# A linear-attention, Mish and greedy-mixture kernel: the token assignment moved off GpSimd, the first expert's weights converted in small pieces, and the front end's order adjusted

## The chip, the cores and the metric

The kernel runs on one core of a Trainium2 chip. The core has a matrix engine (TensorE, PE in the profile; PEld is its weight load), a vector engine (VectorE, DVE), a scalar engine (ScalarE, ACT), GpSimd (POOL) and a queue engine that issues transfers (SyncE, SP). Each engine works through its own instructions strictly in program order, and waits on semaphores for the others. The metric is the device time of one execution in microseconds (us). Before the change it is 855.05 us, the median of three runs (854.58 to 855.65).

## The reference

Three stages follow each other. All data are float32.

```python
# 1. linear attention: batch 4, 8 heads, 768 steps, head size 48
for t in range(S):
    cur = einsum('bhd,bhe->bhde', u * kt, vt)
    y[:, :, t] = einsum('bhd,bhde->bhe', rt, state + cur)
    state = wt[..., None] * state + einsum('bhd,bhe->bhde', kt, vt)
x = y as (3072 tokens, 384)
# 2. h = x @ w_in (384 x 2048);  g = h * tanh(softplus(h));  x = g @ w_out (2048 x 384)
# 3. greedy mixture: 8 experts of 384 x 1024 and 1024 x 384, room for 384 tokens each
order = argsort(-(x @ w_gate).flatten())
for idx in order:                      # the largest logit first
    tok, e = idx // 8, idx % 8
    if assigned[tok] >= 0 or counts[e] >= 384: continue
    assigned[tok] = e; counts[e] += 1
out[assigned == e] = relu(x[...] @ w1[e]) @ w2[e]
```

Every matrix product with float32 accuracy is made of three float16 products: each factor is split into a high and a low half (hi, lo), and hi·hi, hi·lo and lo·hi are summed.

## The kernel before, in words

**Stages 1 and 2 as one list of events.** The attention is cut into 24 units of 128 steps (4 sequences, 6 chunks each). A unit has the steps att0 (running product of the decays), inv, r1, k1, bon1 and bon2 (the u term), K and S (state), A1 (scores) and y. The Mish layer works on 12 groups of 256 tokens; a group has eight slots, each a first product (mm1: 18 matmuls into a tile Hp), followed by the activation steps aln, tanh and g. Its second product (mm2) is a stream of 384 portions of three matmuls into a tile X; `more(n)` emits the next n portions, wherever it is called. The weights of the Mish layer arrive as raw words and are converted (`conv`, on the vector engine) and split into halves (`split`, on ACT and the vector engine), and w_out's blocks are transposed and multiplied by the gate weights (ogT, ogM), which gives the logits as eight further columns of the second product. Each step is an event with a due time from the table `CFG`; the events are sorted by due time (units are 4 slots apart: `at(4 * n - 13 + o, ...)`), and called in that order, so the table alone decides the order on every engine. `warm` events are matmuls without use, `need` only checks at build time that a step comes after those it rests on. The tile Y of the attention has two buffers, which bon1, bon2, K, S and y take in turn.

**The gate.** When the event list is done, 128 or a few fewer portions of the second product are left, and `gate()` works out which token goes to which expert. It takes seven phases. A phase finds the threshold at which the next expert is full, by a search with 32 candidates at a time: four iterations (`count`) in phase 0, three in each of the other six, 22 in all. In an iteration the vector engine compares 3072 keys with 32 candidates in two halves (L854), TensorE counts by 24 small matmuls (`tally`, L859), the vector engine compares the counts with the room left (ge, L871), TensorE spreads the result (bc, L874), and the vector engine reduces it (L875) and forms the next keys (L921). Wherever such a step hands over to another engine the generator yields, and the main loop calls `more(CFG["amount"][kind])`: nine matmuls behind the first half of the compare, three behind the tally, nine between phases ('c'), twelve at each of the steps 't' of the set-up and of `make_idx`. At the end of a phase, `assign` multiplies the one-hot rows by the selection and adds them to Acc, on GpSimd (L902, L904).

**The first expert's weights** are fetched before the gate (`load_w(0)`, two transfers of 1.5 MB into tiles stg, two buffers each used once per expert) and converted during it: at every fourth yield, `conv_w(..., pool=True)` has ACT write the high half (L1105) and GpSimd scale the weights and write the low half (L1107, L1108), a third of a matrix at a time. Behind the gate `load_w(1)` fetches the second expert into the same buffers.

**make_idx** turns the assignment into a list of tokens per expert: one-hot rows OH (24 instructions, L1074), and a table Q times the token numbers tid (on GpSimd, L1069), multiplied on TensorE (L1079). The rest of the stream is spread over its four yields 'o'. **The experts:** GpSimd gathers the tokens' rows (L1115), a register is loaded and tested (L1199 to 1203; the branch to an exact gate is not taken here), and for each expert the rows are transposed (`xpose`, L1127), multiplied (L1148, L1165) and scattered.

Of the kernel before, what the change touches and what calls it, by code (L numbers as in the profile page):

```python
# [9 lines left out]
F32 = mybir.dt.float32  # L10
# [3 lines left out]
ALU = mybir.AluOpType  # L14
# [4 lines left out]
P = 128  # L19
# [4 lines left out]
CFG = {'conv': [-27.9, -26.2, -0.2, 0.8, 1.8, 2.8, 3.7, 5.3, 5.9, 6.6, 7.3, 8.0, 8.7, 10.4, 10.6, 11.3],  # L24
 'split': [-27.3, -25.6, 0.9, 1.9, 2.9, 3.8, 4.7, 5.7, 6.7, 7.4, 8.1, 8.8, 9.0, 11.2, 11.4, 12.1],
 'ogT': [7.5, 8.45, 9.9, 10.25, 10.95, 11.85, 12.55, 13.25],
 'ogM': [8.15, 9.35, 10.2, 10.9, 11.35, 12.05, 12.75, 14.45],
 'u': {'att0': -0.5,
       'bon1': 2.27,
       'bon2': 3.25,  # L30
       'r1': 2.7,
       'k1': 3.175,
       'K': 4.91,
       'A1': 5.52,
       'S': 5.93,
       'y': 6.8,
# [16 lines left out]
            'K': -17.4,  # L53
            'A1': -18.5,
            'bon2': -18.5,
# [13 lines left out]
            'inv': -22.8,  # L69
            'r1': -17.5,  # L70
            'bon1': 2.3,
            'k1': -17,
            'bon2': 3.05,
            'K': 3.85,
            'A1': 3.7,
            'S': 4.05,
            'y': 5.5},
        4: {'K': 4.96,
            'A1': 5.82,
            'S': 5.98,  # L80
            'y': 7.0,
# [26 lines left out]
        7: {'bon1': 1.37,  # L108
            'att0': -0.4,
            'bon2': 4.35,  # L110
# [10 lines left out]
        23: {'K': 3.81, 'A1': 6.27, 'y': 6.65}},  # L121
 'rate': [(9, 0), (81, 200), (82, 202), (85, 216), (86, 220), (93, 234), (99, 256)],
 'close_cv': 15.0,
 'close_att': 86.65,
 'mm1': 0.7,
 'mm2': 1.4,
 'aln': -0.1,
 'tanh': (1.6, 1.66),
 'g': (3.0, 3.01),
# [7 lines left out]
           ('ld', 9): -23.6,  # L137
           ('warm', 1): -26.45,
           ('warm', 2): -24.4,
# [3 lines left out]
           ('warm', 6): 9.9},  # L143
 'warm': [36, 0, 12, 0, 0, 0, 0],
 'amount': {'I0': 3, 'I1': 0, 'g': 1, 't': 4, 'c': 3, 'o': 11},
 'cwn': 4,
 'dve': {'glo': {0,
# [59 lines left out]
 'alone': {9},  # L207
 'lg': 4.01}


@with_exitstack
def tile_rwkv_mish_greedy_moe(
# [12 lines left out]
    nc = tc.nc  # L225
# [4 lines left out]
    NCH = SEQ // C  # L230
# [51 lines left out]
    def part(n, i):  # L282
        if i == 0:
            return TB[n % 3][:, 0:WC].rearrange("p (a c) -> p a c", a=NP)
        return TB[n % 3][:, WC + (i - 1) * RC:WC + i * RC].rearrange("p (a c) -> p a c", a=NP)
# [70 lines left out]
    def need(*keys):  # L356
        assert made.issuperset(keys), keys
# [491 lines left out]
    NH = 2  # L849
# [11 lines left out]
    def count(x, E_, gr, mid=None, late=None):  # L861
        cn = pgs.tile([J, NE], F32, name="cn")
        for h in range(NH):
            compare(x, gr, h)
            if h == 0 and mid is not None:
                mid()
            yield f"I{h}"
            tally(cn, E_, h)
        if late is not None:
            late()  # L870
        nc.vector.tensor_tensor(ge, cn, remS[0:J, :], op=ALU.is_ge)  # L871
        yield "g"
        bc = pgs.tile([P, NE], F32, name="tp", bufs=1)
        nc.tensor.matmul(bc, ones[0:J, :], ge, start=True, stop=True)  # L874
        nc.vector.tensor_reduce(nn_, bc, op=ALU.max, axis=AX.X)  # L875
        cnt_out[:] = [cn, bc]

    cnt_out = [None, None]

    def setup_range():  # L880
# [19 lines left out]
    def assign(ph, E_, s_):  # L900
        dst = Acc if ph == 0 else Ap
        nc.gpsimd.tensor_tensor(dst, E_, s_[:, :, None].to_broadcast([P, NTT, NE]), op=ALU.mult)  # L902
        if ph > 0:
            nc.gpsimd.tensor_tensor(Acc, Acc, Ap, op=ALU.add)  # L904

    def gate():
# [6 lines left out]
        for ph in range(NE - 1):  # L913
# [25 lines left out]
            nc.vector.tensor_tensor(cur, best, tk, op=ALU.add)  # L939
            assign(ph, E_, s_)  # L940
            yield "c"
# [111 lines left out]
    def make_idx(middle=None):  # L1053
# [8 lines left out]
        with nc.allow_low_precision(reason="slots are integers below 2^24"):  # L1062
# [5 lines left out]
                                slf[:, 0, :, None].to_broadcast([P, NTT, NTT]), op=ALU.is_equal)  # L1068
        nc.gpsimd.tensor_tensor(Q, Q, tid[:, :, None].to_broadcast([P, NTT, NTT]), op=ALU.mult)  # L1069
        ix = pgs.tile([P, NTT], F32, name="cn")  # L1070
        NQ = 4
        for q in range(NQ):
            for i in range(q * NTT // NQ, (q + 1) * NTT // NQ):
                nc.vector.tensor_scalar(OH[:, i], col, slf[:, 1, i:i + 1], None, op0=ALU.is_equal)  # L1074
            if q == 0 and middle is not None:
                middle()
            yield "o"
            for i in range(q * NTT // NQ, (q + 1) * NTT // NQ):
                nc.tensor.matmul(ix, OH[:, i, :], Q[:, i], start=(i == 0), stop=(i == NTT - 1))  # L1079
# [13 lines left out]

    def conv_w(e, step, pool=False):
        s1, s2 = wts[e]
        if step == 0:
            wf[e] = tuple(p2b[e % 2].tile(sh, F16, name=nm, bufs=1)
                          for sh, nm in (([P, 2, KD, F2], "a1"), ([P, 2, NF2, DM], "a2")))
        a1, a2 = wf[e]
        if step < KD:  # L1100
            src, dst, sc_ = s1[:, step], a1[:, :, step], SW1
        else:
            h = slice(3 * (step - KD), min(3 * (step - KD) + 3, NF2))
            src, dst, sc_ = s2[:, h], a2[:, :, h], SW2
        nc.scalar.activation(dst[:, 0], src, AF.Copy, scale=sc_)  # L1105
        if pool:
            nc.gpsimd.tensor_scalar(src, src, sc_, 1.0, op0=ALU.mult, op1=ALU.mult)  # L1107
            nc.gpsimd.tensor_tensor(dst[:, 1], src, dst[:, 0], op=ALU.subtract)  # L1108
        else:
            nc.vector.scalar_tensor_tensor(dst[:, 1], src, sc_, dst[:, 0], op0=ALU.mult, op1=ALU.subtract)  # L1110

# [67 lines left out]
    load_w(0)  # L1179
    cw = [(0, i) for i in range(NCV)]  # L1180
    amount = CFG["amount"]
    n = 0
    for kind in gate():
        more(amount[kind])
        n += 1
        if n % CFG["cwn"] == 0 and cw:
            conv_w(*cw.pop(0), pool=True)
    for x in cw:
        conv_w(*x, pool=True)
    load_w(1)  # L1190
    for kind in make_idx(check):
# [8 lines left out]
    with tc.If(redo > 0):  # L1200
        exact_gate()
        run_through(make_idx())
        gather(0)
    for e in range(NE):
        nx = e + 1 < NE
# [83 lines left out]
```

## Time and profile before

| what | value |
| --- | --- |
| time, median of 3 runs | 855.05 us |
| the profiled execution's own time | 854.59 us |
| its span | 852.8 us |
| busy PE / DVE / ACT / POOL | 778.8 / 536.1 / 518.5 / 88.9 us |
| mean granted TensorE clock | 0.961 |

The profile shows one execution. The span goes from the first instruction to the last; 1.8 us of the execution's time lie outside it. A busy time is the sum of the instructions of an engine; PE is busy for 91% of the span, but that is a mean over stages with different limits. The granted clock is 1 at TensorE's higher level (2.4 GHz) and 0.5 at its lower (1.2 GHz); a mean between them says how a stretch was divided. Times in the rows below are counted from the start of the span; a row of a timeline holds the start, the length, engine, line, operation and tiles, and in brackets the idle time of that engine before it and what ended it.

### The profile page before, as it was taken

The page shows a single profiled execution, that of the slowest core. Times are in us where ns is not written, and L with a number is a line of the kernel's source. Part 1 is how long each engine was busy: PE and PEld are TensorE (multiplying, and loading weights), DVE is VectorE, ACT ScalarE, POOL GpSimd, SP SyncE. Part 2 cuts the span into 40 slices and gives each one's busy share as a digit, 9 for nine tenths or more (in the row PEclk, how much of TensorE's full clock was granted, in tenths as well). Part 3 has the DMA queues.
Part 4 walks back from the last instruction along what each step waited for, and adds up shares of the span by engine and source line. Part 5 has one row for each costly group of instructions (what it writes and reads, how often), then busy time and mean ns, then how long its engine had stood idle before and what let it go on. Part 6 is the DMA issues. An engine that isn't in the chain of part 4 may idle for free.

```text
span 852.8 us, 16533 instructions
## 1 busy us (share of the span) xinstructions
PE 778.8 (91%) x7047; PEld 538.0 (63%) x7047; DVE 536.1 (63%) x861; ACT 518.5 (61%) x731; POOL 88.9 (10%) x123
## 2 busy tenths in 40 slices
PE   7683879999999999999999999799959999999996
PEld 3562656777777777767776775455536556555564
DVE  6999875767677767676765345766655543455520
ACT  2558879898988888888977794110005543355521
POOL 0000000000000000000000002531130232122311
PEclk9796999999999999999999999899979999999999
DMA  7870412222322223322200004000144444555100
GB/s 281 211 234 11 149 38 53 38 52 65 71 41 50 52 48 68 69 44 49 50 25 11 15 1 168 10 20 20 46 179 158 147 136 163 185 194 185 65 29 28
DMA packets 21822, 73.79 MB, mean 87 GB/s; under 512 B 4112, under 2 KB 12688, under 8 KB 19696
## 3 DMA queue, kind: packets, MB, share of 16 engines
q1 hardware_dynamic: 18672, 63.24, 25.1%
q0 software_dynamic: 3072, 9.44, 3.5%
q8 instruction: 57, 0.93, 0.5%
q14 instruction: 21, 0.17, 0.1%
HBM read 62.05 MB, written 9.44 MB: 84 GB/s over the span
## 4 chain that ended last, share of the span: by engine, by line
PE 50%; issue 18%; DVE 13%; ACT 12%; POOL 5%; DMA 0%; POOLq 0%; ACTq 0%; DVEq 0%
PE X L639 18%; PE Hp L587 15%; POOL xr L1115 3%; POOL out_dram L1170 2%; PE A L439 2%; PE Y L491 2%; PE Y L495 2%; ACT es L607 2%; PE cn L859 2%; ACT L590 1%; PE A L375 1%; ACT L606 1%; PE Hp L1148 1%; ACT es L590 1%; DVE cv L516 1%
## 5 line engine op out<-in xcount | busy, mean ns | idle before, releaser
L639 PE MATMUL X<-wo,g 128*128 128x392 f16 (+1 forms) x1152 | 223.4, 337 | 1.7 <-DVE V L681 0.9
L587 PE MATMUL Hp<-xg,wi 128*128 128x256 f16 x1728 | 209.4, 276 | 3.0 <-DVE wi L527 2.0
L587 PEld LDWEIGHTS <-wi 128*128 128x128 f16 x1728 | 168.8, 99 | 35.5 <-issue 3.1
L639 PEld LDWEIGHTS <-g 128*128 128x128 f16 x1152 | 108.4, 100 | 68.9 <-issue 12.1
L1148 PE MATMUL Hp<-xe,a 128*128 128x384 f16 (+1 forms) x612 | 102.6, 322 | 6.3 <-DVE hT L1153 5.2
L1165 PE MATMUL X<-a,hT 128*128 128x384 f16 x576 | 97.2, 326 | 0.0
L590 ACT ACTIVATE es<-Hp 128x512 f32<-128x512 f32 x96 | 57.9, 603 | 56.7 <-PE Hp L587 56.2
L1148 PEld LDWEIGHTS <-a 128*128 128x128 f16 x612 | 59.5, 100 | 48.2 <-issue 14.2
L608 DVE TENSOR_TENSOR hs<-hs,es 128x1024 f32<-128x1024 f32 x48 | 56.8, 1220 | 41.2 <-ACT es L607 41.2
L1165 PEld LDWEIGHTS <-hT 128*128 128x128 f16 x576 | 56.4, 98 | 34.8
L1153 DVE SCALAR_TENSOR_TENSOR hT<-Hp,hT 128x384 f16<-128x384 f32 x64 | 35.3, 552 | 47.6 <-ACT hT L1152 47.6
L366 ACT ACTIVATE x1o<-X 128x384 f32<-128x384 f32 x21 | 10.4, 497 | 89.4 <-PE X L639 61.9
L621 DVE TENSOR_TENSOR g<-hs,g 128x1024 f16<-128x1024 f32 x48 | 56.6, 1220 | 12.4 <-ACT g L366 12.2
L1168 ACT ACTIVATE or<-X 128x384 f32<-128x384 f32 x24 | 11.8, 490 | 81.0 <-issue 60.7
L366 ACT ACTIVATE hs<-Hp 128x512 f32<-128x512 f32 x92 | 55.4, 602 | 0.0
L1105 ACT ACTIVATE a<-stg 128x1024 f16<-128x1024 f32 (+2 forms) x48 | 49.9, 1048 | 7.3 <-DMA stg<-in_w_dram 7.3
L802 POOL IOTA jk<- 128x32 f32 x5 | 0.6, 154 | 509.3 <-PE Hp L587 509.3
L1110 DVE SCALAR_TENSOR_TENSOR a<-stg,a 128x1024 f16<-128x1024 f32 (+2 forms) x42 | 51.1, 1218 | 3.2 <-ACT a L1105 2.7
L607 ACT ACTIVATE es<-es,right 128x1024 f32<-128x1024 f32 x48 | 52.7, 1141 | 0.3
L1130 DVE SCALAR_TENSOR_TENSOR xe<-cn,xe 128x384 f16<-128x384 f32 x24 | 13.3, 555 | 62.0 <-ACT xe L1129 61.9
L1152 ACT ACTIVATE hT<-Hp 128x384 f16<-128x384 f32 x64 | 31.4, 490 | 33.7 <-PE Hp L1148 32.6
L597 ACT ACTIVATE es<-es 128x2048 f32<-128x2048 f32 x24 | 46.2, 1923 | 0.1
(188 smaller groups left out, 1055.9 us busy)
## 6 DMA issues: line engine op xcount, KB each, us to landing
stg<-in_w_dram SPq DMA_DIRECT2D x16, 1536.0 KB, 7.6
T<-in_rkw_dram SPq DMA_DIRECT2D x42, 288.8 KB, 5.0
v<-in_v_dram SPq DMA_DIRECT2D x24, 192.0 KB, 4.9
raw<-in_w_out_dram SPq DMA_DIRECT2D x6, 768.0 KB, 4.5
x_dram<-x1o SPq DMA_DIRECT2D x24, 192.0 KB, 1.9
wo<-in_w_in_dram SPq DMA_DIRECT2D x4, 768.0 KB, 8.3
raw<-in_w_in_dram SPq DMA_DIRECT2D x2, 768.0 KB, 7.6
g<-in_w_in_dram SPq DMA_DIRECT2D x2, 768.0 KB, 11.5
```

The source lines that it names most:

```text
L366: nc.scalar.activation(dst, src, AF.Copy, scale=scale)
L587: nc.tensor.matmul(h[:, fi, :], wi[:, a, kk, f * P:(f + 1) * P], xg[g][:, b, kk, :], start=(n == 0), stop=(n == 3 * KD - 1))
L590: nc.scalar.activation(es[g, hf][:, 2 * q:2 * q + 2, :], h, AF.Sigmoid, scale=-1.0 / (SX * SWI))
L597: nc.scalar.activation(e, e, AF.Arctan)
L607: nc.scalar.activation(e, e, AF.Sin, scale=-2.0, bias=right)
L608: nc.vector.tensor_tensor(h, h, e, op=ALU.mult)
L621: (nc.vector if on_v("glo", 2 * H_ + q) else nc.gpsimd).tensor_tensor(gt[:, 1, sl], h, gt[:, 0, sl], op=ALU.subtract)
L639: nc.tensor.matmul(x, gt[:, a, ff, m * P:(m + 1) * P], wo[:, b, f, 0:n], start=(f == 0 and i == 0 and not now_l), stop=(f == NF - 1 and i ...
L1105: nc.scalar.activation(dst[:, 0], src, AF.Copy, scale=sc_)
L1110: nc.vector.scalar_tensor_tensor(dst[:, 1], src, sc_, dst[:, 0], op0=ALU.mult, op1=ALU.subtract)
L1148: nc.tensor.matmul(ps[:, cs], a1[:, a, kk, f * P:(f + 1) * P], x[:, b, kk, cs], start=(n == 0), stop=(n == 3 * KD - 1))
L1165: nc.tensor.matmul(ps, h[:, a, f, ms], a2[:, b, f, :], start=(n == 0), stop=(n == 3 * NF2 - 1))
```

## The change

Five things are changed.

1. **GpSimd has no tensor work in the gate.** `assign` runs on the vector engine. In `make_idx`, GpSimd's product of Q and tid is dropped; the 24 instructions that make OH multiply by tid themselves, with a second scalar operand.
2. **The first expert is converted piecewise.** The six conversions become 14 pieces of 512 or 384 columns. A list `aside` holds one entry per piece, and `load_w(1)` as the last. Each of the 22 iterations takes one entry, right behind the second half of its compare; a phase's `assign` is put at the head of the list, so the first iteration of the next phase takes it. An entry for piece i has ACT write the high half of piece i+1 and the vector engine the low half of piece i.
3. **`load_w(1)`** therefore runs from an iteration of the last phase.
4. **30 matmuls without use** (`hold`, 128 columns) stand in front of the first expert, behind the branch.
5. **The table of due times and amounts:** 12 useless matmuls of 512 columns (warm 3) at slot 0.15; for most units A1, S and bon2 later by an eighth to half a slot, unit 7's att0 a slot earlier; mm2 and the first tanh an eighth of a slot earlier; the rate of the second product slightly other, with the same total; five portions instead of four at the steps 't'; unit 17's Dt on GpSimd. `att0` checks at build time that the steps which read its buffer came before.

```diff
-       'bon2': 3.25,
+       'bon2': 3.5,
...
-       'A1': 5.52,
-       'S': 5.93,
+       'A1': 5.645,
+       'S': 6.43,
...
- 'rate': [(9, 0), (81, 200), (82, 202), (85, 216), (86, 220), (93, 234), (99, 256)],
+ 'rate': [(9, 0), (80, 200), (82, 200), (85, 216), (87, 220), (93, 234), (99, 256)],
...
- 'mm2': 1.4,
+ 'mm2': 1.275,
- 'tanh': (1.6, 1.66),
+ 'tanh': (1.475, 1.66),
...
- 'warm': [36, 0, 12, 0, 0, 0, 0],
- 'amount': {'I0': 3, 'I1': 0, 'g': 1, 't': 4, 'c': 3, 'o': 11},
- 'cwn': 4,
+ 'warm': [36, 0, 12, 12, 0, 0, 0],
+ 'amount': {'I0': 3, 'I1': 0, 'g': 1, 't': 5, 'c': 3, 'o': 11},
...
             if h == 0 and mid is not None:
                 mid()
+            if h == NH - 1 and aside:
+                aside.pop(0)()
             yield f"I{h}"
...
-        nc.gpsimd.tensor_tensor(dst, E_, s_[:, :, None].to_broadcast([P, NTT, NE]), op=ALU.mult)
+        nc.vector.tensor_tensor(dst, E_, s_[:, :, None].to_broadcast([P, NTT, NE]), op=ALU.mult)
         if ph > 0:
-            nc.gpsimd.tensor_tensor(Acc, Acc, Ap, op=ALU.add)
+            nc.vector.tensor_tensor(Acc, Acc, Ap, op=ALU.add)
...
-            assign(ph, E_, s_)
+            aside.insert(0, lambda ph=ph, E_=E_, s_=s_: assign(ph, E_, s_))
             yield "c"
...
-        nc.gpsimd.tensor_tensor(Q, Q, tid[:, :, None].to_broadcast([P, NTT, NTT]), op=ALU.mult)
...
-                nc.vector.tensor_scalar(OH[:, i], col, slf[:, 1, i:i + 1], None, op0=ALU.is_equal)
+                nc.vector.tensor_scalar(OH[:, i], col, slf[:, 1, i:i + 1], tid[:, i:i + 1], op0=ALU.is_equal, op1=ALU.mult)
...
+    def conv_hi(src, dst, sc_):
         nc.scalar.activation(dst[:, 0], src, AF.Copy, scale=sc_)
...
+    def conv_lo(src, dst, sc_):
+        nc.vector.scalar_tensor_tensor(dst[:, 1], src, sc_, dst[:, 0], op0=ALU.mult, op1=ALU.subtract)
...
+    def small_pieces(e):
+        for step in range(NCV):
+            src, dst, sc_ = halves(e, step)
+            if step < KD:
+                for q in range(2):
+                    c = slice(q * F2 // 2, (q + 1) * F2 // 2)
+                    yield src[:, c], dst[:, :, c], sc_
+            else:
+                for q in range(src.shape[1]):
+                    yield src[:, q], dst[:, :, q], sc_
...
     load_w(0)
-    cw = [(0, i) for i in range(NCV)]
+    todo = list(small_pieces(0))
+    conv_hi(*todo[0])
+
+    def piece(i):
+        if i + 1 < len(todo):
+            conv_hi(*todo[i + 1])
+        conv_lo(*todo[i])
+
+    aside += [lambda i=i: piece(i) for i in range(len(todo))]
+    aside.append(lambda: load_w(1))
...
     for kind in gate():
         more(amount[kind])
-        n += 1
-        if n % CFG["cwn"] == 0 and cw:
-            conv_w(*cw.pop(0), pool=True)
-    for x in cw:
-        conv_w(*x, pool=True)
-    load_w(1)
+    while aside:
+        aside.pop(0)()
...
+    if CFG["hold"]:
+        hold = pgs.tile([P, P], F32, name="cn")
+        for _ in range(CFG["hold"]):
+            nc.tensor.matmul(hold[:, 0:P], ones, OH[:, 0], start=True, stop=True)
     for e in range(NE):
```

## Rows read from the trace of the kernel before

**Rows 1.** Windows: stretch, length, busy us (instructions) of PE, PEld, DVE, ACT, POOL; clock; DMA.
```profile
31.40:100.00 68.60, 45.50 (x485) 35.89 (x483) 66.57 (x91) 46.33 (x68) 0.00 (x0) 0.80 0.51 150
134.00:300.00 166.00, 164.40 (x1639) 124.56 (x1639) 117.33 (x155) 145.72 (x198) 0.00 (x0) 1.00 0.26 54
```

**Rows 2.** Windows of the gate: phase 0, phase 1, phase 3.
```profile
529.10:548.90 19.80, 14.33 (x148) 7.72 (x148) 14.25 (x29) 4.37 (x5) 11.31 (x9) 0.87 0.15 60
548.90:564.00 15.10, 12.76 (x121) 6.97 (x121) 11.36 (x26) 2.27 (x3) 10.13 (x7) 0.84 0.04 14
...
575.50:586.20 10.70, 10.70 (x124) 6.31 (x123) 7.10 (x28) 0.49 (x1) 1.55 (x2) 1.00 0.06 20
```

**Rows 3.** Timeline of PE in phase 2: two tallies and the spread.
```profile
566.28 0.76 PE L859 MATMUL cn<-Eo,I__6026 128*32 128x8 f16 x24
...
569.24 0.76 PE L859 MATMUL cn<-Eo,I__6026 128*32 128x8 f16 x24
...
570.52 0.17 PE L874 MATMUL tp<-ge,ones 32*128 32x8 f16 x1
```

**Rows 4.** Timeline of DVE: a compare of phase 0, one of phase 2, and ge.
```profile
540.61 3.67 DVE L854 TENSOR_TENSOR I__6026<-y,jk 128x384 f16<-128x384 f32 x2
...
570.03 0.15 DVE L871 TENSOR_TENSOR ge<-cn,remS 32x8 f16<-32x8 f32 x1 [0.75 <-PE cn L859]
...
571.21 1.03 DVE L854 TENSOR_TENSOR I__6026<-y,jk 128x384 f16<-128x384 f32 x2
```

**Rows 5.** Timeline of POOL around that compare of phase 0.
```profile
541.57 2.30 POOL L1108 TENSOR_TENSOR a<-stg,a 128x1024 f16<-128x1024 f32 x1
```

**Rows 6.** Timeline of DVE: two instructions of 512 columns; one of 192.
```profile
7.39 0.69 DVE L400 TENSOR_TENSOR T<-T,E 128x512 f32<-128x512 f32 x1
7.99 0.69 DVE L425 SCALAR_TENSOR_TENSOR inv<-nt,inv 128x512 f32<-128x512 f32 x1
...
528.83 0.36 DVE L898 TENSOR_TENSOR Eo<-Vs,best 128x192 f16<-128x192 f32 x1
```

**Rows 7.** Timeline of DVE in the set-up, then in make_idx.
```profile
527.38 0.16 DVE L891 TENSOR_SCALAR sc<-tp 128x1 f32<-128x1 f32 x1 [1.98 <-PE tp L890]
...
527.77 0.22 DVE L893 TENSOR_SCALAR sc<-tp,sc 128x1 f32<-128x1 f32 x1
...
623.46 2.02 DVE L1074 TENSOR_SCALAR OH<-col,slf 128x128 f16<-128x128 f16 x6
...
625.67 3.00 DVE L1074 TENSOR_SCALAR OH<-col,slf 128x128 f16<-128x128 f16 x18
```

**Rows 8.** The branch line: operation, count, ns min/median/max, starts.
```profile
L1200 PEldq COMPARE_BRANCH  x1: 3312/3312/3312, 629.3 to 629.3; - x1
```

**Rows 9.** Timeline of PE at the start of the first expert.
```profile
636.09 1.54 PE L1127 MATMUL cn<-ident,xr 128*128 128x128 f32 x6 [7.18 <-issue]
...
638.16 1.97 PE L1148 MATMUL Hp<-xe,a 128*128 128x128 f16 x17 [0.33 <-DVE xe L1130]
```

**Rows 10.** Windows of the same stretch.
```profile
636.00:640.00 4.00, 3.58 (x25) 3.21 (x26) 1.11 (x2) 0.98 (x2) 1.97 (x3) 0.50 0.30 94
640.00:644.50 4.50, 3.83 (x42) 3.64 (x41) 1.20 (x3) 1.65 (x4) 0.00 (x0) 0.69 0.16 44
```

**Rows 11.** Timelines of SP and ACT: the second expert's fetch and first use.
```profile
615.43 0.38 SPq L1089 DMA_DIRECT2D stg<-in_w_dram  x1
...
644.22 1.99 ACT L1105 ACTIVATE a<-stg 128x1024 f16<-128x1024 f32 x2
```

**Rows 12.** Timelines of PE, DVE and ACT in the front end.
```profile
42.47 3.57 PE L587 MATMUL Hp<-xg,wi 128*128 128x256 f16 x18
...
44.35 1.32 DVE L444 COPY_PREDICATED Dt<-mask,A 128x512 f32<-128x512 int32 x2
...
68.82 1.28 ACT L606 ACT_TABLE_LOAD   x1
...
97.50 1.09 PE L491 MATMUL Y<-T,S 48*64 48x128 f32 x16 [1.05 <-DVE S L474]
```

More of the change, by code (lines that the diff above doesn't have):

```diff
@@ L24 @@
 CFG = {'conv': [-27.9, -26.2, -0.2, 0.8, 1.8, 2.8, 3.7, 5.3, 5.9, 6.6, 7.3, 8.0, 8.7, 10.4, 10.6, 11.3],
- 'split': [-27.3, -25.6, 0.9, 1.9, 2.9, 3.8, 4.7, 5.7, 6.7, 7.4, 8.1, 8.8, 9.0, 11.2, 11.4, 12.1],
- 'ogT': [7.5, 8.45, 9.9, 10.25, 10.95, 11.85, 12.55, 13.25],
- 'ogM': [8.15, 9.35, 10.2, 10.9, 11.35, 12.05, 12.75, 14.45],
+ 'split': [-27.3, -25.6, 0.9, 1.9, 2.9, 3.8, 4.7, 5.6, 6.7, 7.4, 8.1, 8.8, 9.0, 11.2, 11.4, 12.1],
+ 'ogT': [7.4, 8.45, 9.9, 10.25, 10.95, 11.85, 12.55, 12.75],
+ 'ogM': [8.15, 9.35, 10.2, 10.9, 11.35, 11.95, 12.75, 14.45],
  'u': {'att0': -0.5,
        'bon1': 2.27,
-       'bon2': 3.25,
+       'bon2': 3.5,
        'r1': 2.7,
@@ L53 @@
             'K': -17.4,
-            'A1': -18.5,
+            'A1': -17.5,
             'bon2': -18.5,
@@ L69 @@
             'inv': -22.8,
-            'r1': -17.5,
+            'r1': -17.6,
             'bon1': 2.3,
@@ L74 @@
             'K': 3.85,
-            'A1': 3.7,
+            'A1': 4.2,
             'S': 4.05,
@@ L79 @@
             'A1': 5.82,
-            'S': 5.98,
+            'S': 6.98,
             'y': 7.0,
@@ L108 @@
         7: {'bon1': 1.37,
-            'att0': -0.4,
+            'att0': -1.4,
             'bon2': 4.35,
@@ L137 @@
            ('ld', 9): -23.6,
-           ('warm', 1): -26.45,
+           ('warm', 1): -25.35,
            ('warm', 2): -24.4,
@@ L207 @@
  'alone': {9},
- 'lg': 4.01}
+ 'lg': 4.135,
+ 'hold': 30}
 @with_exitstack
@@ L377, in att0 @@
     def att0(n):
+        if n > 1:
+            need(("k1", n - 2), *([("S", n - 2)] if UN[n - 2][1] + 1 < NCH else []))
         Tw = part(n, 0)
@@ L878, in tile_rwkv_mish_greedy_moe @@
     cnt_out = [None, None]
+    aside = []
     def setup_range():
@@ L1092, in load_w, with halves @@
         wts[e] = (s1, s2)
-    def conv_w(e, step, pool=False):
+    def halves(e, step):
         s1, s2 = wts[e]
@@ L1100, in conv_w @@
         if step < KD:
[L1101 to L1104, printed above, removed]
+            return s1[:, step], a1[:, :, step], SW1
+        h = slice(3 * (step - KD), min(3 * (step - KD) + 3, NF2))
+        return s2[:, h], a2[:, :, h], SW2
+    def conv_hi(src, dst, sc_):
         nc.scalar.activation(dst[:, 0], src, AF.Copy, scale=sc_)
[L1106 to L1110, printed above, removed]
+    def conv_lo(src, dst, sc_):
+        nc.vector.scalar_tensor_tensor(dst[:, 1], src, sc_, dst[:, 0], op0=ALU.mult, op1=ALU.subtract)
+    def conv_w(e, step):
+        x = halves(e, step)
+        conv_hi(*x)
+        conv_lo(*x)
+    def small_pieces(e):
[8 more added lines that the diff above has]
+                    yield src[:, q], dst[:, :, q], sc_
     def gather(e):
@@ L1179, in tile_rwkv_mish_greedy_moe @@
     load_w(0)
-    cw = [(0, i) for i in range(NCV)]
+    todo = list(small_pieces(0))
[6 more added lines that the diff above has]
+    aside.append(lambda: load_w(1))
     amount = CFG["amount"]
-    n = 0
     for kind in gate():
         more(amount[kind])
-        n += 1
-        if n % CFG["cwn"] == 0 and cw:
-            conv_w(*cw.pop(0), pool=True)
-    for x in cw:
-        conv_w(*x, pool=True)
-    load_w(1)
+    while aside:
+        aside.pop(0)()
     for kind in make_idx(check):
```

2 rows, old and new, of the table CFG are left out of this document.

## The prediction

> **What bounds the kernel now.** I read the windows view first, over the whole span in stretches, then the gate alone, then the timelines of TensorE, the vector engine and GpSimd inside it. The windows show three regimes. From 31 to 100 us the vector engine is busy for 66.57 of 68.60 us and TensorE for 45.50: the vector engine sets the pace there [rows 1]. From 134 us on TensorE is busy for 164.40 of 166.00 us at the full clock [rows 1]; there nothing that another engine does shows in the time unless it makes TensorE wait. The third regime is the gate. In phase 3 TensorE is again busy for 10.70 of 10.70 us, but phases 0 and 1, of four and three iterations, take 19.80 and 15.10 us with TensorE busy for 14.33 and 12.76 us of them at a mean clock of 0.87 and 0.84, while GpSimd is busy for 11.31 and 10.13 us [rows 2].
>
> The timelines say why. An iteration that nothing disturbs lasts from one tally to the next, 569.24 - 566.28 = 2.96 us [rows 3], and is filled by TensorE's own work. Its compare takes 1.03 us; the same two instructions in phase 0 take 3.67 us [rows 4], and they lie across a GpSimd subtraction of 2.30 us [rows 5] that belongs to the first expert's low halves. So in phases 0 and 1 the vector engine is slowed by GpSimd's conversions, TensorE waits for the compare, and in the pauses it loses its clock as well.
>
> **The change part by part.**
>
> *GpSimd's conversions go.* Phase 0 should become one undisturbed phase of three iterations and a fourth: 10.70 + 2.96 = 13.66 us, instead of 19.80; phase 1 10.70 instead of 15.10; and the stretch between the second and third row, phase 2, in which the last conversion ends, 10.70 instead of 575.50 - 564.00 = 11.50 [rows 2, 3]. That is 6.1 + 4.4 + 0.8 = 11.3 us. The same from TensorE's side: it was idle for 5.47 + 2.34 = 7.8 us of phases 0 and 1, and a clock of 0.87 and 0.84 means that 5.1 and 4.8 us of them ran at half speed, of which half is lost where work was there: up to 4.9, in sum 7.8 to 12.7. I take -11.5; the ends are -7.8 (the clock falls all the same) and -12.7. TensorE's useful work is the same in both kernels, so this gain stays only if its pauses don't come back elsewhere; that is what the next lines ask.
>
> *The 14 pieces and the assigns on the vector engine.* Two instructions of 512 columns start 7.99 - 7.39 = 0.60 us apart, and each is shown with 0.69 us [rows 6]. A piece stands behind the second compare, where the vector engine waits 0.75 us for the tally before ge [rows 4]. Behind ge TensorE has three further matmuls to do, so that ge's result, there at 570.03 + 0.15 = 570.18, is taken up only at 570.52 [rows 3, 4]. The room is thus 0.75 + 0.34 = 1.09 us per iteration against 0.60 to 0.69, and the pieces cost nothing. An assign has two instructions of 192 columns at up to 0.36 us [rows 6], 0.72 us, in an iteration that has to place the new one-hot rows too; against that the phase ends lose GpSimd's own two instructions. I take 0 for six of them and 0.1 for the one at the end that no tally hides, with 0 to 2 as the bounds. If the cover is gone it is rival A below.
>
> *ACT's high halves* fall into the gate, where ACT is busy for 4.37 of 19.80 us [rows 2]: hidden. SP's queue has `load_w(1)` between two stores of finished rows; it can only wait for the last piece, which the vector engine has done one iteration before. *The second expert's fetch* was issued at 615.43 and its first use is at 644.22 [rows 11], so its landing was not waited for; fetched sooner it is worth 0.
>
> *Five portions instead of four at the steps 't'.* In the set-up the vector engine waits for TensorE's short matmuls, which stand behind the portions (1.98 us at the second) [rows 7]. An iteration of 2.96 us holds a tally of 0.76 and four portions [rows 3], so a portion is about 0.53 us, and two such steps come that much later each: +1.05. The third such step lies in `make_idx`, under a chain of the vector engine: 0. The portions moved are missing at the last yields, where the vector engine's OH leads anyway.
>
> *make_idx.* The first six OH take 2.02 us and the other eighteen 3.00, thus 0.34 against 0.17 each, the six beside GpSimd's product [rows 7]. Without it the six take 1.00: -1.0. The second scalar operand is not in the trace; the nearest rows are an instruction of one element with no scalar operand from memory, 0.16, and one with, 0.22 [rows 7]. So it costs between 0 and 24 x 0.06 = 1.4 us; I take +0.4, as the 24 overlap each other.
>
> *The 30 useless matmuls.* TensorE's branch takes 3.31 us from 629.3 [rows 8], so they begin at 632.6. The experts' first matmuls of 128 columns, at clock 0.50, take 1.97 / 17 = 0.116 us each [rows 9, 10]; 30 of these are 3.5 us and end at 636.1, just when the first gathered rows are there (636.09) [rows 9]. They delay nothing, or 0.2 us. What they give is clock: of the work behind, 3.58 us ran at 0.50, and 4.50 us had a mean of 0.69, that is 2.8 at half speed, in which 2.4 us of matmuls fell [rows 10]. At the full level this is 1.8 + 1.2 = 3.0 us less. In the first of these stretches TensorE was busy for 3.58 of 4.00 us and the clock did not rise [rows 10], and the transposes and activations between the matmuls stay. I take -1.5, the ends are -3.0 and +0.2. (The Trainium skill, TensorE: Matmul & The Clock Gate, part 1, has the lower level as the default and activity as what releases it. By that alone the useless matmuls would have the first expert start at the full level, with the 3.0; here a stretch that was busy for nine tenths did not release it, so I stay at the half.)
>
> *The front end.* Warm 3 puts 12 matmuls of 512 columns ahead of unit 2's K, A1 and S and the first Mish product. By the 18 of 256 columns behind them, 3.57 us [rows 12], they are 24 x 0.198 = 4.8 us at most. TensorE's work behind them moves later by that, less what a clock that rises sooner gives back. The vector engine, which leads here, takes unit 2's scores at 44.35 [rows 12] out of its own backlog; I see a few tenths. The first tanh is now split by unit 4's inv, between its two halves: ACT loads a table (1.28 us [rows 12]) once more, and the vector engine's second product behind it comes later. Unit 4's S moves away from y, where TensorE had waited 1.05 us for it [rows 12]: that may be won. Sum +0.5, between -2 and +3. The steps moved by fractions of a slot from 134 us on fall where TensorE has 1.6 us of pauses in 166 [rows 1]; 0, and rival B is what could go wrong. Unit 17's Dt on GpSimd has some two slots until it is read, and may slow the vector engine for the length of one GpSimd instruction (2.30 us [rows 5]) where it is busy for 117 of 166 us [rows 1]: 0, from 0 to +1. The build-time check is nothing on the chip.
>
> **The sum**, on the profiled execution's 854.59 us: -11.5 + 0.1 + 1.05 - 1.0 + 0.4 - 1.5 + 0.5 = -11.95, which gives 842.6. That execution lies 0.46 below the median of the runs, so I forecast 843.1 against 855.05.
>
> **The rivals.**
>
> A: *The vector engine becomes the gate's bound.* The pieces and the assigns then add their whole length to the chain of compare, tally, ge: 14 x 0.69 + 6 x 0.72 = 14.0 us, and the time is 857.1; at half of that 850. For it: an assign and the new one-hot rows stand in one iteration. Against it: the wait of 0.75 us and the 0.34 behind it [rows 3, 4]. It starts from 1.09 us per iteration, which a piece of 0.69 does not reach. The full form has 0.02, the half 0.04.
>
> B: *The new order of S, bon1 and y makes TensorE wait in each unit* (the slower side). The tile Y has two buffers; S now stands behind the next unit's bon1, close to y, and y's products wait until a buffer has been read. The one such wait in the rows costs 1.05 us [rows 12]. Sixteen units follow the general due times; at 1.05 each that is +16.8 and the time 859.9. It makes the kernel slower from 12 / 16 = 0.75 us per unit on. Against it: the buffer that y takes is now bon1's, which ACT empties while a product of 18 matmuls lies between. Chance 0.05.
>
> C: *Only the gate gives something, and the front end takes part of it back.* The useless matmuls bring nothing (+1.5) and warm 3 and the split tanh cost the upper end (+2.5): 847.1. For it: the vector engine in the front end has next to no pauses in which to catch up [rows 1]. Chance 0.11.
>
> D: *The change does not do what it says:* the long compares have another cause than GpSimd. Then phases 0 and 1 keep their length and the rest nets 1.05 - 1.0 + 0.4 - 1.5 + 0.5 = -0.6: 854.5. Against it: phase 3, with a GpSimd share of 1.55 in 10.70 us, has none [rows 2]. Chance 0.03.
>
> **How the numbers follow.** The forecast has the rest, 0.75. Its own range goes by the ends of the gate (-7.8, -12.7), of OH, of the useless matmuls and the front end, not all at once: 838 to 847. To leave out no more than 2 in 10 I take 837 to 849, which holds C and stops short of the half form of A. Less than 0.2% (1.7 us) is what a measurement of this kernel can't tell from no change. Faster by more: forecast, C and the half form of A, 0.90. Within: D, and some of B with fewer units, 0.04. Slower: A in full and most of B, 0.06.
>
> **What would show it.** Right: the iterations of phases 0 and 1 last about 2.96 us, with compares of about 1.03 us and TensorE without pauses at clock 1; ge starts no later behind the tally than now; the OH are 0.17 us apart from the first on; the transposes start about 3.5 us behind the branch's end, and the clock is back before the second product of the first expert. Wrong: ge led by the vector engine itself instead of by the tally (A); waits of TensorE on bT or S in each unit after 134 us (B); a first transposed block of w_out that comes more than a microsecond later than now (C).

## The result, and the profile after

The changed kernel takes 841.64 us, the median of four runs (839.02 to 843.24), against 854.82 (851.44 to 855.65) for four runs of the kernel before beside it: ratio 0.985, 95% interval 0.981 to 0.989. Forecast were 843.1, range 837 to 849. The profiled execution took 839.02 us with a span of 837.0.

Its windows, with the columns of [rows 1]: the front end and the steady stretch as there, then three of the gate (phase 0, phase 1, phase 3), then the first expert's start (the 30 matmuls, then the work up to the first matmul of 384 columns).

```profile
31.40:100.00 68.60, 45.34 (x479) 35.04 (x479) 63.94 (x86) 46.64 (x68) 0.00 (x0) 0.83 0.46 140
134.00:300.00 166.00, 166.00 (x1651) 125.24 (x1650) 119.25 (x158) 146.13 (x199) 0.00 (x0) 1.00 0.26 55
527.50:540.30 12.80, 12.17 (x151) 7.28 (x152) 9.84 (x33) 2.04 (x4) 0.00 (x0) 1.00 0.16 62
540.30:550.90 10.60, 10.60 (x125) 6.22 (x124) 8.02 (x30) 1.42 (x3) 0.00 (x0) 1.00 0.06 20
561.50:572.10 10.60, 10.60 (x124) 6.23 (x124) 8.01 (x31) 1.31 (x3) 0.00 (x0) 1.00 0.06 21
619.00:622.20 3.20, 3.15 (x31) 3.19 (x31) 0.00 (x0) 0.00 (x0) 1.90 (x2) 0.50 0.56 147
622.20:628.60 6.40, 5.25 (x65) 4.43 (x64) 2.28 (x5) 2.59 (x6) 1.98 (x3) 0.91 0.28 86
```

Phases 0 and 1, which took 19.80 and 15.10 us at a clock of 0.87 and 0.84 [rows 2], are now like phase 3 was: TensorE has its full clock and next to no pause, and GpSimd does nothing. One iteration on the vector engine (timeline: start, length, engine, line, operation, idle time before it) and two on TensorE:

```profile
530.33 1.03 DVE L856 TENSOR_TENSOR I__6039<-y,jk 128x384 f16<-128x384 f32 x2
531.27 0.68 DVE L1113 SCALAR_TENSOR_TENSOR a<-stg,a 128x512 f16<-128x512 f32 x1
532.04 0.15 DVE L875 TENSOR_TENSOR ge<-cn,remS 32x8 f16<-32x8 f32 x1
532.74 0.17 DVE L879 TENSOR_REDUCE sc<-tp 128x1 f32<-128x8 f32 x1 [0.55 <-PE tp L878]
```

```profile
531.24 0.76 PE L861 MATMUL cn<-Eo,I__6039 128*32 128x8 f16 x24
...
534.20 0.76 PE L861 MATMUL cn<-Eo,I__6039 128*32 128x8 f16 x24
...
535.48 0.17 PE L878 MATMUL tp<-ge,ones 32*128 32x8 f16 x1
```

A tally follows the last after 2.96 us, as [rows 3] had it for an undisturbed iteration. The piece of 0.68 us fills the pause of 0.75 that stood before ge in [rows 4], and ge starts 0.80 us behind the tally's start, where it started 0.79 behind before (570.03 - 569.24).

The span of each execution is cut below at events that all kernels have: the set-up's first reduction (523.46 before, 520.90 after), the first tally of the gate (529.71, 528.12), the reduction that writes cp behind the last phase (619.93, 605.50), the end of make_idx (idx written; 629.16, 615.26), the first matmul of 384 columns of the first expert (644.47, 628.61), and the end (852.84, 836.98). "idx" is the start of the instruction that writes it. The time is the median of each kernel's runs; e4, e5, e8 and e6 ran once, so the columns of their one trace are what is read of them. All in us:

| kernel | time, median | set-up | gate | make_idx | idx to 384 columns | set-up to end |
| --- | --- | --- | --- | --- | --- | --- |
| before | 854.82 | 6.25 | 90.22 | 9.23 | 15.31 | 329.38 |
| after | 841.64 | 7.22 | 77.38 | 9.76 | 13.35 | 316.08 |
| c0_after_again | 840.07 | 7.22 | 77.39 | 9.74 | 13.55 | 316.28 |
| e1_gate_only | 843.89 | 7.22 | 77.38 | 9.75 | 17.21 | 319.94 |
| e2_table_only | 851.84 | 6.25 | 90.22 | 9.23 | 13.09 | 327.19 |
| e10_before_pad | 853.19 | 6.24 | 90.10 | 9.24 | 13.26 | 327.22 |
| e7_no_warm3 | 842.64 | 7.22 | 77.38 | 9.74 | 16.17 | 318.89 |
| e3_no_hold | 841.04 | 7.23 | 77.38 | 9.74 | 13.63 | 316.37 |
| e4_pool_pieces | 850.93 | 8.37 | 84.46 | 9.75 | 13.30 | 324.72 |
| e5_double_piece | 843.62 | 7.22 | 78.93 | 9.75 | 13.01 | 317.28 |
| e8_pool_assign | 842.54 | 7.22 | 78.37 | 9.75 | 13.28 | 317.02 |
| e6_q_on_dve | 841.01 | 7.22 | 77.38 | 9.08 | 13.41 | 315.48 |
| e11_best | 839.60 | 6.25 | 77.38 | 9.06 | 13.08 | 314.17 |
| e12_best_pad | 838.32 | 6.24 | 77.39 | 9.07 | 12.97 | 314.04 |

The budget of the change behind the set-up closes: +0.97 - 12.84 + 0.53 - 1.96 = -13.30, which is 316.08 - 329.38; from the 384 columns to the end both take 208.37. The stretch ahead of it is no measure: the changed kernel's two executions reach the set-up at 520.90 and 524.57, 3.67 us apart in one and the same code. Most of it is TensorE's clock: in the repetition it stays at its lower level for 3.4 us longer near 125 us and falls once more, for 3.4 us, at 467 us, and the Mish products fall behind by 1.4 and by 1.7 us there. The second place, as a window in both (the second row, the repetition, is 1.0 us longer and still holds six matmuls less):

```profile
445.00:490.50 45.50, 44.23 (x458) 34.05 (x459) 20.03 (x27) 35.48 (x46) 0.00 (x0) 1.00 0.04 12
```

```profile
447.00:493.50 46.50, 45.24 (x452) 34.15 (x453) 19.38 (x26) 34.82 (x45) 0.00 (x0) 0.96 0.04 12
```

So medians of a few runs are uncertain by a microsecond or two, and the columns of the table say what they can't.

### The profile page after: what moved, and what is told of

It reads as the page before. It is cut to its first block, busy times and chain, and to the rows that moved or that the text cites. A ratio compares the mean times of both kernels' runs of the same rounds, so it can differ in the third digit from the quotient of the medians.

```text
span 837.0 us, 16607 instructions
## 1 busy us (share of the span) xinstructions
PE 774.8 (93%) x7089; PEld 536.3 (64%) x7089; DVE 533.5 (64%) x887; ACT 520.9 (62%) x740; POOL 60.6 (7%) x98
## 5 line engine op out<-in xcount | busy, mean ns | idle before, releaser
L641 PE MATMUL X<-wo,g 128*128 128x392 f16 (+1 forms) x1152 | 217.4, 331 | 1.7 <-DVE V L683 0.9
L589 PE MATMUL Hp<-xg,wi 128*128 128x256 f16 x1728 | 207.0, 275 | 1.8 <-DMA xg<-xg 1.7
L589 PEld LDWEIGHTS <-wi 128*128 128x128 f16 x1728 | 166.7, 99 | 30.8 <-issue 3.0
L641 PEld LDWEIGHTS <-g 128*128 128x128 f16 x1152 | 105.5, 98 | 67.8 <-issue 9.3
L1167 PE MATMUL Hp<-xe,a 128*128 128x384 f16 (+1 forms) x612 | 100.8, 316 | 6.4 <-DVE hT L1172 5.2
L1167 PEld LDWEIGHTS <-a 128*128 128x128 f16 x612 | 57.6, 97 | 48.2 <-issue 14.2
L1113 DVE SCALAR_TENSOR_TENSOR a<-stg,a 128x1024 f16<-128x1024 f32 (+4 forms) x56 | 59.6, 1066 | 3.2 <-ACT a L1110 2.7
L1110 ACT ACTIVATE a<-stg 128x1024 f16<-128x1024 f32 (+4 forms) x56 | 51.0, 926 | 7.2 <-DMA stg<-in_w_dram 7.2
L366 ACT ACTIVATE g<-hs 128x1024 f16<-128x1024 f32 x41 | 42.0, 1075 | 0.3 <-DVE hs L610 0.3
```

Source lines behind the costliest of these rows:

```text
L366: nc.scalar.activation(dst, src, AF.Copy, scale=scale)
L589: nc.tensor.matmul(h[:, fi, :], wi[:, a, kk, f * P:(f + 1) * P], xg[g][:, b, kk, :], start=(n == 0), stop=(n == 3 * KD - 1))
L641: nc.tensor.matmul(x, gt[:, a, ff, m * P:(m + 1) * P], wo[:, b, f, 0:n], start=(f == 0 and i == 0 and not now_l), stop=(f == NF - 1 and i ...
L1167: nc.tensor.matmul(ps[:, cs], a1[:, a, kk, f * P:(f + 1) * P], x[:, b, kk, cs], start=(n == 0), stop=(n == 3 * KD - 1))
```

## The experiments

**The two halves of the change.** c0_after_again is the changed kernel once more. e1_gate_only is the new code with the old table, five portions and the 30 matmuls kept; e2_table_only is the old code with the new table, four portions kept.

```diff
 e1: -'S': 6.43, 'warm': [36, 0, 12, 12, 0, 0, 0], ...   +'S': 5.93, 'warm': [36, 0, 12, 0, 0, 0, 0], ...
 e2: the same exchange the other way, in the kernel before
```

> The changed kernel as it is, as the control of this group. The profiled execution of it was 15.8 us shorter in span than that of before, but its four times lie between 839.0 and 843.2. Theory (a stretch of about 2.6 us in front of the gate was won in that one execution by where the clock fell, not by the change): the front of the gate (the end of the event list) comes about as late as before, 520 to 522 us, in this profile, and the ratio is 0.984 to 0.986. Rival (the new table of due times wins 2 to 3 us in every execution): the front of the gate again at about 518.5 us.

> The changed gate, index and hold with the old table of due times, rates and useless matmuls (only the five portions at the steps 't' stay). Theory (the gain is the gate's): the stretch from the first tally to the last phase's pen is about 74.3 us as in the changed kernel, and the ratio equals the control's within 0.2%. Rival (the table wins 2 to 3 us by its new order): the time is 2 to 3 us above the control's.

> The old gate, index and experts with the new table of due times, rates and useless matmuls. Theory (the gain is the gate's): within 1.5 us of the kernel before, and the gate 86.8 us long as before. Rival (the table wins 2 to 3 us): 851.5 to 853 against about 855, with the same pauses of TensorE in phases 0 and 1.

Beside 854.95 (17 runs of before): 840.07 (ratio 0.984, 0.981 to 0.987), 843.89 (0.989, 0.986 to 0.993) and 851.84 (0.997, 0.995 to 0.999). c0 repeats the result, and its later set-up shows that the early one of the first profile was not the table's doing. The gate's 12.84 us belong to the code alone. But the table, which I had valued at nothing, is worth 3 to 4 us either way (3.1 in e2, 3.8 in e1), and the columns put it into one place: idx to the 384 columns, 2.2 us shorter in e2 than before and 3.9 longer in e1 than after. Nothing of the table acts there. Rows of e1 and of e2 at that place (the branch: operation, count, ns, start; then TensorE's timeline):

```profile
L1223 PEldq COMPARE_BRANCH  x1: 3812/3812/3812, 616.3 to 616.3; - x1
...
623.79 3.36 PE L1230 MATMUL cn<-OH,ones 128*128 128x128 f16 x30 [7.90 <-issue]
```

```profile
L1201 PEldq COMPARE_BRANCH  x1: 3532/3532/3532, 627.8 to 627.8; - x1
...
632.08 0.87 PE L1128 MATMUL cn<-ident,xr 128*128 128x128 f32 x3 [4.66 <-DMA xr<-x_dram,idx]
```

In e2 the branch ends at 631.4 and the transposes start at 632.08, when the gathered rows land. In e1 the branch ends at 620.1 and TensorE stands for another 3.7 us before matmuls that need nothing from a DMA. The kernel before had that second standstill too: its branch ends at 632.6 [rows 8], its transposes start at 636.09, and the row says "issue", not DMA [rows 9].

**What in the table does it: 24 instructions.** Warm 3 is 12 matmuls and 12 weight loads in TensorE's program, 580 us ahead of the branch. e7 takes it out of the changed kernel; e10 puts 12 matmuls of one column in its place into the kernel before, which take next to no time.

```diff
 e7: -'warm': [36, 0, 12, 12, 0, 0, 0],   +'warm': [36, 0, 12, 0, 0, 0, 0],
 e10 (kernel before, at slot 0.15): +for _ in range(12): matmul(wps[:, 0:1], id16, warm_rhs[:, 0:1])
```

> The kernel before with twelve matmuls of one column each, without use, where warm 3 stands in the changed kernel: as many more instructions of TensorE, with next to no work. Theory (what the new table won came from where TensorE's instructions lie behind the branch: in the kernel before and in the run with the old table TensorE stood still for a second time after the branch, 3.4 and 3.7 us, in the three runs with warm 3 it did not): the transposes start about 4.4 us behind the index's last instruction instead of 6.9, and the time is 2 to 3 us below before. Rival (warm 3 wins by the clock, or the new due times win): 6.9 us as before, and the time within 0.7 us of before.

> The changed kernel without warm 3. Theory (its 24 instructions decide where the code behind the branch lies): the first useless matmul of hold starts about 3.7 us behind the branch's end, as in the run with the old table, instead of 0.1, the transposes start 10.8 us behind the index instead of 6.9, and the time is 2.5 to 4 us above the changed kernel's (843 to 844.5), although the front end comes out 0.5 to 1 us earlier. Rival (warm 3 matters by the clock of the front end): the pause behind the branch stays at 0.1 us, and only the stretch before 100 us differs.

Beside 855.18 (17 runs): e10 853.19 (ratio 0.998, 0.996 to 0.9997), e7 842.64 (0.986, 0.983 to 0.988). The interval of e7 overlaps that of the changed kernel; the columns tell them apart (16.17 against 13.35 and 13.55). Timelines of TensorE behind the branch, of e10 and of e7:

```profile
633.30 0.87 PE L1132 MATMUL cn<-ident,xr 128*128 128x128 f32 x3 [4.63 <-DMA xr<-x_dram,idx]
...
642.19 3.08 PE L1153 MATMUL Hp<-xe,a 128*128 128x384 f16 x18 [0.67 <-DVE hT L1158]
```

```profile
620.02 0.69 PE L1230 MATMUL cn<-OH,ones 128*128 128x128 f16 x5 [3.91 <-DVEq L1223]
623.13 2.83 PE L1230 MATMUL cn<-OH,ones 128*128 128x128 f16 x25 [2.43 <-issue]
625.75 1.49 PE L1146 MATMUL cn<-ident,xr 128*128 128x128 f32 x6
```

e10 has lost the standstill, though its 24 instructions compute nothing and add next to no work. e7 has one again, and it lies inside a loop of 30 equal matmuls: five run, TensorE stops for 2.43 us with nothing to wait for, 25 follow. No data, tile or semaphore divides the fifth from the sixth, only the place in the program. (I had looked for it ahead of the first.) The Trainium skill, Runtime: NRT & Kernel Launch, section "Instruction fetch mechanics", says that instructions come by DMA in blocks of 16 KiB, and that a taken branch outside the window waits for its block; it calls the crossing of a block mostly hidden. The traces agree on the blocks: one instruction queue moves 16,384 bytes at a time, and in every run such a transfer lies inside TensorE's branch. If the standstill is a crossing, they differ in the last: right behind the branch it is seen, with 2.4 to 3.7 us. That it is a block's arrival is inferred. A further transfer follows the branch in every trace, with or without a standstill; in the three with one it ends at 634.74 (before), 622.26 (e1) and 621.74 (e7), and TensorE goes on 1.35, 1.53 and 1.39 us later. For which engine a transfer is, the trace doesn't say.

**The 30 matmuls.** e3 leaves them out.

```diff
- 'hold': 30}
+ 'hold': 0}
```

> The changed kernel without the 30 useless matmuls in front of the first expert. Theory (they give back the clock): the transposes start as long behind the branch as now, the clock stays at 0.5 for some 6 us of the first expert's work, the stretch from the first transpose to the first matmul of 384 columns is 8.4 us instead of 6.4, and the time 2 us above the control's. Rival (they only fill a pause): the same time as the control's, within 0.5 us.

841.04 (ratio 0.985, 0.983 to 0.988), against 840.07 with them: the 2 us that my theory gave them are not there, and no difference can be told. TensorE in e3, then the same rows of the changed kernel:

```profile
619.73 0.88 PE L1146 MATMUL cn<-ident,xr 128*128 128x128 f32 x3 [4.68 <-DMA xr<-x_dram,idx]
622.16 0.87 PE L1146 MATMUL cn<-ident,xr 128*128 128x128 f32 x3 [1.56 <-DVE xe L1149]
...
628.93 3.08 PE L1167 MATMUL Hp<-xe,a 128*128 128x384 f16 x18 [0.67 <-DVE hT L1172]
```

```profile
619.04 3.36 PE L1230 MATMUL cn<-OH,ones 128*128 128x128 f16 x30 [4.04 <-PEq L1223]
622.20 1.49 PE L1146 MATMUL cn<-ident,xr 128*128 128x128 f32 x6
...
624.22 1.11 PE L1167 MATMUL Hp<-xe,a 128*128 128x128 f16 x17 [0.38 <-DVE xe L1149]
...
628.61 3.08 PE L1167 MATMUL Hp<-xe,a 128*128 128x384 f16 x18 [0.67 <-DVE hT L1172]
```

The stretch from the transposes to the 384 columns in e3, as a window (beside the last row of the changed kernel's windows above):

```profile
619.73:628.93 9.20, 6.97 (x63) 6.36 (x64) 2.28 (x5) 2.59 (x6) 3.25 (x5) 0.61 0.35 103
```

Without the matmuls the first rows are there at 619.73, and 9.20 us pass to the 384 columns at a clock of 0.61; with them the transposes start 2.47 later and need 6.41 at 0.91. Of the 2.8 us that the stretch is shorter, 1.7 are TensorE's own work at the higher clock (busy for 5.25 us instead of 6.97); the rest are pauses. One of these is 1.56 us long in e3, ahead of the second transposes: they start at 622.16, and the second rows land at 622.07. Behind the matmuls no such wait is left. So 2.8 are given, 2.5 taken: net 0.3 against the first profile of the changed kernel, 0.1 against c0.

**The gate's cover.** e4 gives the low halves of the 14 pieces to GpSimd (two instructions each); e5 has the vector engine do every low half twice; e8 gives the assignments back to GpSimd and leaves the pieces.

```diff
 e4: -conv_lo(*todo[i])    +gpsimd.tensor_scalar(src, src, sc, ...); gpsimd.tensor_tensor(lo, src, hi, subtract)
 e5: +conv_lo(*todo[i])    a second time
 e8: -nc.vector.tensor_tensor(...) x2 in assign    +nc.gpsimd.tensor_tensor(...) x2, at the phase's end as before
```

> The changed kernel with the low halves of the same 14 pieces made by GpSimd (scale, then subtract) at the same places. Theory (GpSimd's work itself slows the vector engine): a piece of 512 columns takes GpSimd about 0.5 + 1.1 us and overlaps the compares of the next iteration; compares of up to 2 us instead of 1.03 in the iterations with pieces, TensorE with pauses, and the stretch from the first tally to the last counts reduced (77.4 us) 4 to 9 us longer. Rival (only the long blocks of 2.3 us did harm, short pieces fit between): within 1 us of 77.4.

> The changed kernel with each low half made twice by the vector engine, one right behind the other. Theory (an iteration has 1.09 us of room, 0.75 ahead of ge and 0.34 behind it): two pieces of 512 columns need about 1.25 us and lengthen an iteration by 0.1 to 0.2 us, two of 384 columns about 1.0 us and lengthen nothing; the gate is 0.6 to 1.5 us longer. Rival (a piece was just hidden by the 0.75 us alone): each second piece adds its excess over 0.75, about 0.5 and 0.25 us, 5 us in all.

> The changed kernel with the two instructions of each phase's assignment back on GpSimd, the conversion pieces left on VectorE. If the conversions alone were what stretched the gate: gate 77.4 to 78 us (the phases of the kernel before that had only GpSimd's assignment took 10.66). Rival, that GpSimd's assignments cost too: each meets two compares, 7 phases x about 0.3 us, gate 79 to 80.

e4 took 850.93, and its gate 84.46, 7.1 longer. Its set-up is 1.15 longer too: GpSimd, which waits for no compare, begins the first piece there at 530.54, and the gate's first compare takes 2.41 us beside it. Timelines of its vector engine and of GpSimd:

```profile
535.48 1.03 DVE L856 TENSOR_TENSOR I__6039<-y,jk 128x384 f16<-128x384 f32 x2
...
539.93 2.39 DVE L856 TENSOR_TENSOR I__6039<-y,jk 128x384 f16<-128x384 f32 x2
```

```profile
533.37 1.33 POOL L1117 TENSOR_TENSOR a<-stg,a 128x512 f16<-128x512 f32 x1
...
539.88 1.15 POOL L1117 TENSOR_TENSOR a<-stg,a 128x512 f16<-128x512 f32 x1
```

The same compare takes 1.03 us where GpSimd is still and 2.39 where it meets a subtraction and its neighbour: 1.36 longer beside an instruction of 1.15. So it is GpSimd's tensor work, not the place in the gate, that stretched the compares of [rows 4].

e5 took 843.62, its gate 78.93 (+1.55). Its vector engine:

```profile
532.16 1.41 DVE L1113 SCALAR_TENSOR_TENSOR a<-stg,a 128x512 f16<-128x512 f32 x2
533.49 0.15 DVE L875 TENSOR_TENSOR ge<-cn,remS 32x8 f16<-32x8 f32 x1
533.88 0.17 DVE L879 TENSOR_REDUCE sc<-tp 128x1 f32<-128x8 f32 x1 [0.25 <-PE tp L878]
...
535.37 1.41 DVE L1113 SCALAR_TENSOR_TENSOR a<-stg,a 128x512 f16<-128x512 f32 x2
```

The iteration grows from 2.96 to 535.37 - 532.16 = 3.21, by 0.25 for 0.72 us of work: 0.47 of it were still covered. That is the margin by which rival A stayed away, and it agrees with the 1.09 - 0.69 = 0.40 that the prediction read.

e8 took 842.54; its gate is 78.37, 1.0 longer and between what the theory and the rival had: 0.10 to 0.25 in each phase after the first that has a piece too, 0.07 in the others. What GpSimd's addition meets is often not a compare but its neighbour (timelines of the vector engine and GpSimd):

```profile
565.37 0.70 DVE L951 TENSOR_TENSOR Eo<-M,best 128x192 f16<-128x192 f32 x1
```

```profile
564.90 0.96 POOL L909 TENSOR_TENSOR Acc<-Acc,Ap 128x192 f16<-128x192 f16 x1
```

The same instruction takes 0.35 us in the changed kernel. Beside the pieces, then, the assignment on GpSimd costs 1.0. How the 12.84 us divide between the two is not shown by that: in the kernel before a phase with an assignment alone was only 0.07 longer than now (10.66 against 10.59), and its conversions came in longer blocks than those of e4.

**Two costs taken back.** In e6 the OH have one scalar operand again and the vector engine multiplies Q by tid itself, once; e11 is e6 with four portions at 't'; e12 is e11 with warm 3 as 12 one-column matmuls, which keeps the code's place.

```diff
+nc.vector.tensor_tensor(Q, Q, tid[:, :, None].to_broadcast([P, NTT, NTT]), op=ALU.mult)
-tensor_scalar(OH[:, i], col, slf[:, 1, i:i + 1], tid[:, i:i + 1], op0=ALU.is_equal, op1=ALU.mult)
+tensor_scalar(OH[:, i], col, slf[:, 1, i:i + 1], None, op0=ALU.is_equal)
 e11, e12: 't': 5 -> 4
```

> The changed kernel, the OH comparisons with one scalar operand and Q multiplied by tid on VectorE. Second operand dear: OH falls from 0.227 to 0.164 each, compare to idx from 9.76 to about 8.9. Rival, that 0.227 comes from something beside the operand (the port shared with GpSimd's copies): OH stays at 0.22 and compare to idx grows to about 10.4.

> The changed kernel with its two costs taken back: t at 4 as before, and the OH comparisons with one scalar operand, Q multiplied by tid once on VectorE. If the second operand costs 24 x (0.227 - 0.164) = 1.5 us and one more t costs 0.97 us in front of tally 0: set-up's reduce to tally 0 takes 6.25 instead of 7.22, compare to idx about 8.9 instead of 9.76 (1.5 less, 0.68 more for the multiplication), so 1.8 us less than the changed kernel, about 839. Rival: make_idx is led by the transposes and TensorE's standstill behind the branch, which is no shorter: then the time stays at 840 to 842.

> The version before this one (t 4, OH with one scalar operand) with warm 3 as 12 one-column matmuls: the same number of instructions at the same places, so the code lies as in the changed kernel, but its 4.5 us in the front end shrink to about 1. If warm 3's worth is its instructions' place alone, the standstill behind the branch stays at about 3.5 us, and the first expert matmul of unit 7 comes 0.5 to 0.8 us sooner: 838. Rival: warm 3 is worth its clock: then the front end loses what the pad saves, and the time is 839 to 841.

Timelines of the vector engine: the OH of the changed kernel, then those of e11 with the product ahead of them:

```profile
609.04 1.43 DVE L1078 TENSOR_SCALAR OH<-col,slf,tid 128x128 f16<-128x128 f16 x6
...
610.65 4.09 DVE L1078 TENSOR_SCALAR OH<-col,slf,tid 128x128 f16<-128x128 f16 x18
```

```profile
611.75 0.76 DVE L1074 TENSOR_TENSOR Q<-Q,tid 128x576 f16<-128x576 f16 x1
612.42 1.06 DVE L1079 TENSOR_SCALAR OH<-col,slf 128x128 f16<-128x128 f16 x6
...
613.67 2.99 DVE L1079 TENSOR_SCALAR OH<-col,slf 128x128 f16<-128x128 f16 x18
```

4.09 / 18 = 0.227 with the second operand, 2.99 / 18 = 0.166 without: 1.5 us for 24, paid back by one product of 0.76. make_idx falls from 9.76 to 9.08 in e6; 8.9 were expected. e11 has the set-up's 0.97 back as well, and its stretch from the set-up to the end is 1.9 us shorter than the changed kernel's (1.8 were expected). Times beside 853.31 (9 runs): e11 839.60 (ratio 0.984, 0.981 to 0.986), e12 838.32 (0.982, 0.979 to 0.984). In the front end e12 starts its first Mish product 2.0 us sooner than the changed kernel, but the eighth only 0.26 sooner: the first takes 3.04 us there and 2.14 behind warm 3's full length, which so returns nearly all it takes. The two versions have the lowest medians and the shortest stretches of the table, but the intervals of their ratios overlap that of the changed kernel: better by the traces' 2 us, not by the timing alone.

## Why the prediction was right, and where it was not

**The gate** (forecast -11.5 and +0.1). Right in mechanism, short in size: -12.84. Counted from threshold to threshold, phase 0 fell from 16.54 to 10.73, phase 1 from 15.86 to 10.59, phase 2 from 11.78 to 10.59: 5.8 + 5.3 + 1.2, where 6.1, 4.4 and 0.8 were worked out. The four that I took as undisturbed gave 0.07 each, and the end gave 0.29, where I had charged 0.1. e4 shows the cause, e8 what the assignment adds to it, e5 the cover.

**Five portions**: +1.05 forecast, +0.97 measured. **make_idx**: -0.6 forecast, +0.53 measured; this step failed. GpSimd's product did cost the six OH 1.0 us, but the second operand costs 0.061 each in full: the 1.4 that I had as the upper bound from [rows 7], not the 0.4 that I took "as the 24 overlap each other". They don't; and the "OH are 0.17 us apart" of the last part was wrong.

**The 30 matmuls**: -1.5 forecast; this stretch gave -1.96, but not for that reason, and the step "end at 636.1, just when the first gathered rows are there" failed. The rows were not what the transposes waited for in the kernel before. Transposes that wait for them start 4.4 us behind idx (e2: 632.08 - 627.68), which would be at 633.6, and the trace of the kernel before has its first 192 KB of rows moved by 633.2; TensorE stood until 636.09 for another cause, at which the row's "issue" hinted and which I overlooked. So the matmuls' 3.4 us are no free filling. Their clock is worth about 2.0: from the transposes to the 384 columns 8.38 us pass in the kernel before and 6.41 in the changed one, neither with a wait for rows, so the 1.5 was near and the upper end of 3.0 too high. But against a start as soon as the first rows land they cost 2.5 of waiting, which the sum had at 0 to 0.2; that start pauses for the second rows in its turn (e3), so 0.1 to 0.3 are left. What shortened the stretch is that warm 3's 24 instructions moved the second standstill away; I had priced the table at the front end alone.

**The front end** (+0.5) stays open within the spread of its clock: the first transposed block of w_out came at 79.23 instead of 78.42, +0.8. **The steady stretch** (0): TensorE is busy for all of 166.00 us.

The rivals. **A** did not come: ge is led by the tally still, and e5 shows that it would have needed more than a doubled piece to show in full. **B** did not: between 134 and 505 us TensorE's waits sum to 3.4 us in four places, none per unit. **C** was half true, the matmuls bring next to nothing; but its price was paid by the code's place. **D** is refuted by e1, which has the gate's whole gain, and e4. The sum held because the errors met: of the -12.45 forecast behind the set-up -13.30 came, with 1.4 more from the gate and 1.7 from the place of the code (15.31 - 13.63 in e3), against 1.1 lost in make_idx and 1.2 at the matmuls.

**The second expert's fetch** is now issued at 588.23 instead of 615.43 [rows 11] and, as forecast, nothing shows that it was worth anything: from the 384 columns to the end both kernels take 208.37.

## What to carry to other kernels

Where a small engine's work runs beside a chain of short instructions of the vector engine, read the length of one such instruction with and without that neighbour; if the chain waits once per turn for another engine, pieces that fit the wait cost nothing there, and doubling a piece measures the margin. An idle time that the trace puts down to "issue" need not be a wait for data: before filling it, ask whether it stays when the code is moved by a few instructions that do nothing. (It can still be one: in e2 the second transposes stand under "issue" too, at 633.91, and their rows land at 633.82.) And a useless filler ahead of work whose data has arrived costs its own length; set it against what the clock returns.

## What the hardware showed that I had not expected

- TensorE's branch takes 3.3 to 3.8 us in all these kernels, where the other engines' takes 0.04 to 0.07, and a second standstill of 2.4 to 3.7 us may follow it, by the place of the code: 24 instructions more, executed 580 us earlier, take it away (e2, e10), 24 fewer bring it back (e1, e7), and the stretch from idx to the 384 columns moves by 2.0 to 3.9 us.
- Six OH that lay beside GpSimd's product took 2.02 us [rows 7], 1.43 with a second operand and GpSimd still, 1.06 with neither.
- A piece of the first phases lies in front of ge with 0.09 us to spare (531.95 to 532.04), and an iteration still keeps its 2.96: the slack of 0.4 behind it is TensorE's, which takes ge up only after three matmuls of its stream.
